# Row 0 of a fused attention and feed-forward kernel: two interleaved halves, masks added to the scores in PSUM, constants, casts and loads dealt out anew

## The chip, the cores and the metric

The kernel runs on one NeuronCore of a Trainium2 chip. The core has TensorE (PE, with its weight loads written PEld), VectorE (DVE), ScalarE (ACT), GpSimd (POOL) and SyncE (SP), and 16 DMA engines. Times are device microseconds (us) of one execution; lower is better. The number of a kernel is the median of its runs.

## The reference, cut to what matters

Eight batch rows of 576 tokens go through attention with 8 heads of width 64. Heads 0 to 3 see a plain window of 32 tokens back, heads 4 to 7 see every fourth token of the last 128. The result, 4608 tokens of width 512, goes through a feed-forward layer of width 2048 with a squared ReLU.

```python
scores = np.matmul(q, k.transpose(0, 1, 3, 2)) / np.sqrt(D)      # B, H, S, D = 8, 8, 576, 64
rel = pos[:, None] - pos[None, :]
mask_plain = (rel >= 0) & (rel < 32)                             # heads 0..3
mask_dil = (rel >= 0) & (rel < 128) & (rel % 4 == 0)             # heads 4..7
scores = np.where(masks[None], scores, -1e9)
attn = softmax(scores); x = np.matmul(attn, v)                   # -> 4608 tokens x 512
h = np.maximum(x @ w_in, 0.0)                                    # 512 -> 2048
out = (h * h) @ w_out                                            # 2048 -> 512, float32
```

All inputs and the output are float32 in DRAM; the kernel computes with float16 operands and accumulates in float32.

## The kernel before, in words

The feed-forward layer is done in nine chunks of 512 tokens. A chunk needs the transposed attention output `xT` of its tokens, so chunk c needs attention rows up to c. The order of all instructions is written out by hand: `pending` holds generators that emit feed-forward matmuls a few at a time, and `pump(n)` emits the next n pieces between two pieces of attention. Each engine then works through its own queue in that order.

Attention row 0 has no feed-forward work to go with it. Its q and k of the sliding heads are loaded as float32 into `sq` (q on SP's queue, k on ACT's, 1.5 KB runs), its q and k of the dilated heads through POOL's DMA queue, which casts to float16 on the way, straight into `nd_`, its v into `sv` and `sd`. The steps after that: casts (`cast_sliding_qk`), transposes on PE and copies out of PSUM (`t_sliding`, `t_dilated`), scores (`s_sliding`, `s_dilated`), exp on ACT and a multiplication with a 0/1 mask on DVE (`softmax`), the product with v and the normalization (`av_sliding`, `av_dilated`, `normalize`), and transposes into `xT` (`x_sliding`, `x_dilated`). `idle_matmuls` on a zero tile `zz` (14 wide ones at the start, then 5 narrow ones at each step) fill PE's time. Row 0 is laid out as whole tiles of 576 columns; its second half (`av_dilated(0, 1, a)`, `x_sliding(0, 1)`, `x_dilated(0, 1)`) is put between the first pieces of chunk 0.

Chunk 0 is done in two parts in its first layer (`mm1_part_gen`, tokens 0 to 287 at L302, then 288 to 511), and row by row in its second (`mm2_by_rows_gen`, L345). Attention row 1 runs inside chunk 0, with the same steps as row 0: its casts at L145 and L147, then transposes and scores, then `cast_v`, then `attn_values`. The chunks 1 to 8 are `moe_gen`: `mm1_gen` (L324) and a Strassen form of the second layer (`mm2_strassen_gen`, L374); the rows 2 to 7 run inside them, with q and k of those rows first copied to DRAM as float16 (`keep_qk`, L184) and then transposed by DMA on SP's queue (`transpose_by_dma`, L194 and L196) into `QKTx` and `QKTd`.

The loads of row 1 and of the weights are held back: `load_w_in` (two pieces of 1 MB, L128) after the third step of row 0, `load_sliding_qk(1)` and `load_dilated_qk(1)` after the last step that reads row 0's tiles, `load_w_out` (four pieces of 0.5 MB, L135) after the first part of chunk 0's first layer, `reload_v(1)` (L106, L113, L114) after that part, `keep_qk(2)` after row 1's scores. What holds them back is a memset of a part of the tile that is to be loaded, or of the scratch column `hold`, at the wanted place of an engine's queue. The pool `pa` has two PSUM tiles (scores and products with v take turns in them), the pool `pm` four.

The masks are built at L220 to L231, other constants at L232 to L246.

Of the kernel before, what the change touches and what calls it, by code (L numbers as in the profile page):

```python
# [17 lines left out]
def kernel(  # L18
# [58 lines left out]
    QKTp = const.tile([P, 2, 2, PADP + S], FP16, name="QKTp")  # L77
# [9 lines left out]
    early = tp.tile([QB, 2, 2, 12 * D * 2], FP16, name="early", tag="T")  # L87
    nq_ = early[:, 0].rearrange("p i (j h d) -> p i j h d", j=6, h=HH)
    nd_ = early[:, 1].rearrange("p i (g x) -> p i g x", g=2)
# [12 lines left out]
    def load_sliding_v(b):  # L102
        for m in range(NB):
            lo = QB * m - PADP
            p0 = PADP if m == 0 else 0
            nc.sync.dma_start(  # L106
                out=sv[p0:P, m, :, :],
                in_=v[b, 0:HH, lo + p0 : lo + P, :].transpose([1, 0, 2]),
            )

    def load_dilated_v(b, eng):
        vv = v[b, HH:H].rearrange("h (i c) d -> i h (c d)", c=DIL)
        eng.dma_start(out=sd[PADD:P, 0, :, :], in_=vv[0:QD])  # L113
        eng.dma_start(out=sd[:, 1, :, :], in_=vv[QD - PADD : CL])  # L114
# [11 lines left out]
    def load_w_in():  # L126
        for f0, f1 in ((0, 1024), (1024, 2048)):
# [5 lines left out]
    def load_w_out():  # L133
        for j in range(4):
# [23 lines left out]

    def cast_sliding_v(eng, step, m0=0, m1=NB):
        for m in range(m0, m1, step):  # L160
            copy(eng, vp[:, m : m + step, :, 0:D], sv[:, m : m + step, :, :])

    def cast_dilated_v(eng, step):
        for t in range(2):
# [37 lines left out]
    load_sliding_qk(0, (nc.sync, nc.scalar))  # L202
# [7 lines left out]
    nc.vector.memset(sd[0:64, 0, :, :], 0.0)  # L210
    nc.scalar.activation(warm, warm, ACTF.Exp)
    load_dilated_qk(0)
    make_identity(nc, ident)
    load_sliding_v(0)
    load_dilated_v(0, nc.scalar)
# [4 lines left out]
    for m, w, pad in ((maskp, QB, PADP), (maskd, QD, PADD)):  # L220
# [6 lines left out]
        nc.vector.tensor_mul(  # L227
            m.rearrange("p (n w) -> p n w", w=w),
            lo_[:, 0:w].unsqueeze(1).to_broadcast([P, UW // w, w]),
            hi_[:, 0:w].unsqueeze(1).to_broadcast([P, UW // w, w]),  # L230
        )  # L231
    nc.vector.memset(QKTp[:, 1, :, 0:PADP], 0.0)  # L232
    nc.vector.memset(QKTx[:, 1, 0:PADP], 0.0)
    nc.vector.memset(QKTd[:, 1, :, 0:KPAD], 0.0)
    nc.vector.memset(AT[:, :, UW:640], 0.0)

    nc.vector.memset(vp[:, :, :, D : D + 1], 1.0)
    nc.vector.memset(vp[0:PADP, 0, :, D : D + 1], 0.0)
    nc.vector.memset(vd[:, 1, :, :, D : D + 1], 1.0)
    nc.vector.tensor_scalar(  # L240
        out=vd[:, 0, :, :, D],
        in0=relf[:, 0:1].unsqueeze(2).to_broadcast([P, DIL, HH]),
        scalar1=-PADD + 0.5,
        scalar2=None,
        op0=ALU.is_lt,
    )  # L246
# [249 lines left out]
    def t_sliding(b, hp, i, wide=False):  # L496
        p_ = pt(f"pt{b}_{hp}_{i}", wide)
        for j in range(6):
# [7 lines left out]
            QKTp[:, i, hp, PADP:].rearrange("x (p j) -> x p j", j=6),  # L506
# [19 lines left out]

    def softmax(u, ps, mask):
# [3 lines left out]
    def s_sliding(b, hp):  # L531
        tiles = [pa(f"ps{b}_{hp}_{half}") for half in range(2)]
        for half, ps in enumerate(tiles):
            for m3 in range(3):
                m = 3 * half + m3
                for e in range(2):
# [3 lines left out]
                        QKTp[r, 1, hp, QB * m : QB * m + P],  # L540
                        QKTp[r, 0, hp, PADP + QB * m : PADP + QB * (m + 1)],
# [43 lines left out]
    def normalize(b, what, pav, w):  # L585
        x = xp.tile([QB, 2, HH, D], FP16, name=f"x{b}_{what}", tag="x")
        rcp = xp.tile([QB, 2, HH], FP32, name=f"rcp{b}_{what}", tag="rcp")
        pv = pav[0:w, :, 0 : HH * (D + 2)].rearrange("p i (h d) -> p i h d", d=D + 2)
        nc.vector.reciprocal(rcp[0:w], pv[:, :, :, D])
        nc.vector.tensor_tensor(  # L590
            out=x[0:w],
            in0=pv[:, :, :, 0:D],
            in1=rcp[0:w].unsqueeze(3).to_broadcast([w, 2, HH, D]),
            op=ALU.mult,
        )
        return x

    def av_sliding(b, mp):
        pav = pa(f"pav{b}_{mp}")
        for i in range(2):  # L600
            m = 2 * mp + i
# [12 lines left out]
        return normalize(b, f"p{mp}", pav, QB)  # L614

    def av_dilated(b, t, a):
        pav = pa(f"paw{b}_{t}_{a}")
        for e in range(2):
            for h in range(HH):
                off = e * 288 + a * 144 + t * QD  # L620
                nc.tensor.matmul(  # L621
                    pav[:, e, h * (D + 2) : h * (D + 2) + D + 1],
                    AT[:, 4 + h, off : off + P],
# [6 lines left out]
    def x_sliding(b, half, xs, wide):  # L630
        px = pt(f"px{b}_{half}", wide)
        for m3 in range(3):
            m = 3 * half + m3
            x = xs[m // 2][:, m % 2].rearrange("p h d -> p (h d)")
# [12 lines left out]
    def x_dilated(b, t, xs, wide):  # L647
        py = pt(f"py{b}_{t}", wide)
        for a in range(2):
            for e in range(2):  # L650
                x = xs[a][:, e].rearrange("p h d -> p (h d)")
# [30 lines left out]
    def attn_values(b, fill, wide=False):  # L682
        xs = []
        for mp in range(3):
            xs.append(av_sliding(b, mp))
# [3 lines left out]
        ys = [av_dilated(b, 0, 0)]  # L689
# [3 lines left out]
        ys.append(av_dilated(b, 0, 1))  # L693
        fill()
        zs = []
        for a in range(2):
            zs.append(av_dilated(b, 1, a))
# [7 lines left out]
    cast_sliding_qk(0, (nc.scalar, nc.scalar, nc.vector, nc.gpsimd))  # L705
    pj = pmool.tile([P, TOKC], FP32, name="pj", tag="pm")
    idle_matmuls(pj, 14, TOKC)

    def idle():
        idle_matmuls(pj, 5, P)  # L710

    def idle_and_load():
        idle()
        n_idle[0] += 1
        if n_idle[0] == 3:

            nc.vector.memset(hold, 0.0)
            nc.gpsimd.memset(hold, 0.0)
            load_w_in()
            cast_sliding_v(nc.gpsimd, 2)  # L720

    n_idle = [0]
    transposes_and_scores(0, idle_and_load)
    scores_dilated(0, idle)
    cast_dilated_v(nc.scalar, DIL)
    xs = [av_sliding(0, 0)]
    idle()
    xs.append(av_sliding(0, 1))

    nc.vector.memset(sq[:, :, :, 0:1], 0.0)  # L730
    nc.vector.memset(nd_[:, :, :, 0:1], 0.0)
    idle()
    ys = [av_dilated(0, 0, 0)]
    idle()
    x_sliding(0, 0, xs, False)
    idle()
    ys.append(av_dilated(0, 0, 1))
    idle()
# [124 lines left out]
```

The softmax here doesn't subtract the row's maximum and nothing guards it: scores larger than these inputs give would overflow.

## Time and profile before

| | us |
|---|---|
| median of 11 runs | 307.21 (306.31 to 308.09) |
| the profiled execution, its own time | 307.57 |
| its span, from the first to the last instruction | 305.8 |
| PE busy | 294.5 (96%) |
| DVE busy | 213.8 (70%) |
| ACT busy | 184.7 (60%) |
| POOL busy | 42.2 (14%) |
| first matmul of chunk 0's first layer (L302) starts at | 23.75 |
| first matmul of chunk 1's first layer (L324) starts at | 63.47 |

A profile line of the timeline gives the start, the busy time in us, the engine, the line of the kernel, the operation, its output and inputs with shapes, the count, and in brackets how long the engine was idle before it and on what. A line of a table by stage gives the length of the stage, then for each engine the busy time and the number of instructions, then the clock that PE was granted (1.00 is full speed), the share of DMA engine time and GB/s. A line of a DMA queue gives packets, MB written, and the time of the packets as a share of the 16 engines' time. DMA sizes are those of the destination; a load that casts float32 to float16 reads twice as much.

### The profile page before, as it was taken

To read this page: it belongs to the slowest core of one execution; us is meant where nothing else is said; L and a number is where in the kernel's file an instruction comes from. 1 tells how busy PE (TensorE), PEld (TensorE's weight loads), DVE (VectorE), ACT (ScalarE), POOL (GpSimd) and SP (SyncE) were. 2 spreads that over 40 slices of the span, in tenths; PEclk is the share of its full clock that TensorE was granted. 3 is DMA by queue.
4 is the path that set the end of the run, shared out by engine and by line. 5 is a ranking of instruction groups with operands and counts; after the bars stand their busy time and mean duration, and the time that the engine had idled before them with its cause. 6 is when DMAs were issued, how large, how long until landed. Compare 5 with 4: busy or idle time off the path is not lost.

```text
span 305.8 us, 7069 instructions
## 1 busy us (share of the span) xinstructions
PE 294.5 (96%) x2920; PEld 198.1 (65%) x2920; DVE 213.8 (70%) x428; ACT 184.7 (60%) x317; POOL 42.2 (14%) x86
## 2 busy tenths in 40 slices
PE   7789999999899999999999999999999999999995
PEld 2777774444696469646974597459745974684484
DVE  5496772579975797669776977697769775834744
ACT  2586983768924893489438943894389536405710
POOL 4422302006003200320032002300100010000000
PEclk9799999999999999999999999999999999999999
DMA  7999899799899989899859993988420012003004
GB/s 186 245 212 241 143 187 241 165 223 272 206 178 250 263 115 230 238 196 186 192 146 211 168 226 117 223 197 190 118 77 2 0 52 87 2 0 140 0 0 139
DMA packets 83313, 47.91 MB, mean 157 GB/s; under 512 B 67793, under 2 KB 79569, under 8 KB 82897
## 3 DMA queue, kind: packets, MB, share of 16 engines
q1 hardware_dynamic: 75060, 26.12, 40.8%
q0 software_dynamic: 6848, 19.80, 28.5%
q10 hardware_dynamic: 1372, 1.54, 1.8%
q8 instruction: 23, 0.38, 0.5%
q14 instruction: 10, 0.07, 0.1%
HBM read 39.85 MB, written 16.52 MB: 184 GB/s over the span
## 4 chain that ended last, share of the span: by engine, by line
PE 86%; DMA 6%; ACT 3%; SPq 2%; DVE 1%; issue 1%; DVEq 0%; ACTq 0%
PE ph L324 37%; PE pob L374 9%; PE poa L374 9%; PE poe L374 5%; PE poc L374 5%; PE pod L374 5%; DMA sv<-in_v_dram 3%; PE paw L621 3%; PE ph L302 3%; SPq L106 2%; DMA sq<-in_k_dram 2%; PE pav L607 2%; PE py L654 2%; PE pj L474 2%; PE pz L575 1%; PE px L636 1%
## 5 line engine op out<-in xcount | busy, mean ns | idle before, releaser
L324 PE MATMUL ph<-xT,wi 128*128 128x512 f16 x512 | 115.8, 379 | 0.0
L290 ACT ACTIVATE rt<-ph 128x512 f16<-128x512 f32 x128 | 75.4, 601 | 32.9 <-PE ph L324 32.6
L324 PEld LDWEIGHTS <-wi 128*128 128x128 f16 x512 | 48.2, 98 | 55.0
L294 DVE TENSOR_TENSOR g<-rt 128x1024 f16<-128x1024 f16 x56 | 38.7, 691 | 35.2 <-ACT rt L290 34.9
L374 PEld LDWEIGHTS <-sm 128*128 128x128 f16 x512 | 46.9, 98 | 4.9
L374 PEld LDWEIGHTS <-g 128*128 128x128 f16 x384 | 35.8, 98 | 6.5 <-DVE g L292 1.1
L374 PE MATMUL pob<-T,sm 128*128 128x256 f16 x256 | 32.5, 272 | 0.0
L374 PE MATMUL poa<-wo,g 128*128 128x256 f16 x256 | 32.1, 273 | 0.0
L660 ACT COPY xT<-py 128x576 f16<-128x576 f16 x16 | 10.2, 639 | 25.8 <-PE py L654 25.6
L394 POOL DMA_DIRECT2D out_dram<-otl x6 | 4.5, 753 | 152.3 <-DVE otl L429 152.3
L590 DVE TENSOR_TENSOR x_d<-paw,rcp_d 72x512 f16<-72x512 f32 x32 | 22.0, 687 | 1.1
L528 ACT ACTIVATE AT<-pz 128x576 f16<-128x576 f32 x32 | 19.1, 650 | 2.3 <-PE pz L575 1.8
L528 ACT ACTIVATE AT<-ps 128x576 f16<-128x576 f32 x32 | 19.2, 658 | 0.4
L642 ACT COPY xT<-px 128x576 f16<-128x576 f16 x16 | 10.3, 641 | 14.6 <-PE px L636 14.6
L529 DVE TENSOR_TENSOR AT<-AT,maskp 128x576 f16<-128x576 f16 x32 | 15.2, 480 | 3.4 <-ACT AT L528 2.4
L302 PE MATMUL ph<-xT,wi 128*128 128x288 f16 (+1 forms) x128 | 16.6, 272 | 0.9 <-ACT xT L660 0.5
L590 DVE TENSOR_TENSOR x_p<-pav,rcp_p 96x512 f16<-96x512 f32 x24 | 16.5, 686 | 0.8
L529 DVE TENSOR_TENSOR AT<-AT,maskd 128x576 f16<-128x576 f16 x32 | 14.1, 456 | 3.4 <-ACT AT L528 2.5
L374 PE MATMUL poc<-T,sm 128*128 128x256 f16 x128 | 16.2, 272 | 0.0
L374 PE MATMUL pod<-T,g 128*128 128x256 f16 x128 | 16.2, 272 | 0.0
L374 PE MATMUL poe<-wo,sm 128*128 128x256 f16 x128 | 16.1, 273 | 0.0
L345 PE MATMUL po<-wo,g 128*128 128x512 f16 x64 | 16.1, 379 | 0.0
(99 smaller groups left out, 368.4 us busy)
## 6 DMA issues: line engine op xcount, KB each, us to landing
sv<-in_v_dram SPq DMA_DIRECT2D x40, 128.0 KB, 4.2
sd<-in_v_dram SPq DMA_DIRECT2D x7, 512.0 KB, 5.8
dk<-in_k_dram POOLq DMA_DIRECT2D x12, 288.0 KB, 6.3
dk<-in_q_dram POOLq DMA_DIRECT2D x12, 288.0 KB, 7.6
out_dram<-otl POOLq DMA_DIRECT2D x6, 512.0 KB, 3.5
out_dram<-otu POOLq DMA_DIRECT2D x6, 512.0 KB, 3.7
wi<-in_moe_w_in_dram POOLq DMA_DIRECT2D x2, 1024.0 KB, 12.6
wo<-in_moe_w_out_dram POOLq DMA_DIRECT2D x4, 512.0 KB, 10.1
```

The lines of the kernel that those rows point to most:

```text
L290: nc.scalar.activation(rt[:, o, :], ph[:], ACTF.Relu)
L294: nc.vector.tensor_mul(g[:, ffc - 1 : ffc + 1, :], rt, rt)
L302: nc.tensor.matmul(ph[:, 0 : t1 - t0], wi[:, dmk, ffc * P : ffc * P + P], xs[:, dmk, :], start=(dmk == 0), stop=(dmk == NDM - 1),)
L324: nc.tensor.matmul(ph, wi[:, dmk, ffc * P : ffc * P + P], xs[:, dmk, :], start=(dmk == 0), stop=(dmk == NDM - 1),)
L345: nc.tensor.matmul(po, g[:, ffc, t * P : (t + 1) * P], wo[:, ffc, :], start=(ffc == 0), stop=(ffc == NFF - 1),)
L374: nc.tensor.matmul(acc, lhs[:, k, t * P : (t + 1) * P], rhs[:, k, :], start=(first and k == 0), stop=(k == NK - 1), skip_group_check=True,)
L528: nc.scalar.activation(AT[:, u, 0:UW], ps[:, :, 0 : UW // 2], ACTF.Exp, scale=scale)
L529: nc.vector.tensor_mul(AT[:, u, 0:UW], AT[:, u, 0:UW], mask)
L590: nc.vector.tensor_tensor(out=x[0:w], in0=pv[:, :, :, 0:D], in1=rcp[0:w].unsqueeze(3).to_broadcast([w, 2, HH, D]), op=ALU.mult,)
L621: nc.tensor.matmul(pav[:, e, h * (D + 2) : h * (D + 2) + D + 1], AT[:, 4 + h, off : off + P], vd[:, t, 2 * a + e, h, 0 : D + 1], start=Tru ...
L642: nc.scalar.copy(xT[:, 0:2, t0 : t0 + 288], px[:, 0:UW].rearrange("x (c t) -> x c t", c=2),)
L660: nc.scalar.copy(xT[:, 2:4, t0 : t0 + 288].rearrange("x c (i r) -> x c i r", r=DIL), py[:, 0:UW].rearrange("x (c r i) -> x c i r", c=2, r= ...
```

## The change

Row 0 is cut into two halves of 288 tokens (index f). Each half has its own loads, casts, transposes, scores and products, and the halves are interleaved by hand; all of row 0 now comes before chunk 0. Chunk 0's first layer is done with `mm1_gen`, 512 columns wide, instead of two parts.

The masks of row 0 are no longer multiplied in. For each score tile two matmuls of the identity with `biasp` or `biasd` (0 where the mask is 1, -30000 where it is 0) write PSUM first, the scores are accumulated on top, and ACT's exp gives zero. Rows 1 to 7 keep the multiplication.

Some constants (zeros of `sd` and `QKTd`) are written by ACT, others (`constants()`) come later on DVE; casts of v and one cast of q go to POOL. `w_in` is loaded in four pieces of 512 columns, two after POOL's cast of q and two after its casts of v. The loads of row 1, the rest of `w_out` and `keep_qk(2)` are held back by POOL alone: `landed(x)` is a POOL copy of one element of what a DMA wrote. Row 1's scores of the sliding heads and its dilated transposes move from the first into the second layer of chunk 0.

```diff
+    def load_sliding_qk_half(i, f, eng):
+        eng.dma_start(out=sq[:, i, :, 192 * f : 192 * (f + 1)], in_=...)   # runs of 768 B
+    def load_dilated_qk_half(f):
+        for i, src in ((1, k), (0, q)):
+            s4 = src[0, HH:H, 288 * f : 288 * (f + 1), :].rearrange("(g e) (p j) d -> e p g (j d)", e=2, j=8)
+            for e in range(2):
+                nc.gpsimd.dma_start(out=ndh[36 * e : 36 * (e + 1), f, i, :, :], in_=s4[e])
...
-    def load_w_in():
-        for f0, f1 in ((0, 1024), (1024, 2048)):
+    def load_w_in(j0, j1):
+        for f0, f1 in [(512 * j, 512 * (j + 1)) for j in range(j0, j1)]:
             nc.gpsimd.dma_start(out=wi[:, :, f0:f1], in_=moe_w_in[:, f0:f1]...)
...
-    load_sliding_qk(0, (nc.sync, nc.scalar))
+    load_sliding_qk_half(0, 0, nc.sync)
+    load_sliding_qk_half(1, 0, nc.scalar)
...
-    nc.vector.memset(sd[0:64, 0, :, :], 0.0)
     nc.scalar.activation(warm, warm, ACTF.Exp)
-    load_dilated_qk(0)
+    for hh in range(0, HH, 2):
+        nc.scalar.copy(sd[0:PADD, 0, hh : hh + 2, :], zz[0:PADD]...)
+    nc.scalar.copy(QKTd[:, 1, 0, :], zz[:, 0:1].to_broadcast([P, KPAD + S]))
+    nc.scalar.copy(QKTd[:, 1, 1, :], zz[:, 0:1].to_broadcast([P, KPAD + S]))
+    load_dilated_qk_half(0)
+    load_sliding_v(0, 0, 3)
+    load_dilated_v(0, nc.sync, (0,))
+    load_sliding_qk_half(1, 1, nc.sync)
+    load_sliding_qk_half(0, 1, nc.sync)
+    load_dilated_v(0, nc.sync, (1,))
+    load_sliding_v(0, 3, 6)
     make_identity(nc, ident)
-    load_sliding_v(0)
-    load_dilated_v(0, nc.scalar)
+    load_dilated_qk_half(1)
...
+        nc.vector.tensor_mul(m[:, 0:w], lo_[:, 0:w], hi_[:, 0:w])
+        nc.vector.tensor_scalar(out=bias..., in0=m..., scalar1=30000.0, scalar2=-30000.0, op0=ALU.mult, op1=ALU.add)
...
+    def biased(name, bias):
+        ps = pa(name)
+        for e in range(2):
+            nc.tensor.matmul(ps[:, e, 0 : UW // 2], ident, bias, start=True, stop=False, skip_group_check=True)
+        return ps
+    def exp_only(u, ps):
+        nc.scalar.activation(AT[:, u, 0:UW], ps[:, :, 0 : UW // 2], ACTF.Exp, scale=scale)
...
-    idle_matmuls(pj, 14, TOKC)
+    idle_matmuls(pj, 18, TOKC)
+    cast_sliding_qk_half(1, 0, nc.scalar)
+    cast_sliding_qk_half(0, 0, nc.vector)
+    t_sliding_half(0, 0, nc.scalar)
+    t_sliding_half(1, 0, nc.vector)
+    constants()
+    idle(8)
+    t_dilated_half(1, 0, nc.scalar)
+    s_sliding_half(0, 0)
+    s_sliding_half(1, 0)
+    idle(16)
+    t_dilated_half(0, 0, nc.vector)
+    idle(12)
+    s_dilated_half(0, 0)
+    s_dilated_half(0, 1)
+    t_dilated_half(1, 1, nc.scalar)
+    t_dilated_half(0, 1, nc.scalar)
+    cast_sliding_v(nc.gpsimd, 3, 0, 3)
+    cast_dilated_v(nc.gpsimd, DIL, (0,))
+    xs = av_sliding(0, 0, 2)
+    idle(8)
+    ys = av_dilated(0, 0, 0)
+    ys += av_dilated(0, 0, 1)
+    xs += av_sliding(0, 2, 3)
+    cast_sliding_qk_half(1, 1, nc.scalar)
+    cast_sliding_qk_half(0, 1, nc.gpsimd)
+    load_w_in(0, 2)
+    idle(8)
+    s_dilated_half(1, 0)
+    t_sliding_half(0, 1, nc.scalar)
+    t_sliding_half(1, 1, nc.vector)
+    s_dilated_half(1, 1)
+    idle(6)
     x_sliding(0, 0, xs, False)
     x_dilated(0, 0, ys, False)
+    s_sliding_half(0, 1)
+    s_sliding_half(1, 1)
+    cast_dilated_v(nc.gpsimd, DIL, (1,))
+    cast_sliding_v(nc.gpsimd, 3, 3, 6)
+    load_w_in(2, 4)
+    idle(8)
+    zs = av_dilated(0, 1, 0)
+    zs += av_dilated(0, 1, 1)
+    xs += av_sliding(0, 3, 5)
+    xs += av_sliding(0, 5, 6)
+    idle(12)
+    x_dilated(0, 1, zs, False)
+    idle(16)
+    x_sliding(0, 1, xs, False)
+    idle(12)
+    load_w_out(0, 1)
+    landed(wi[:, NDM - 1, 1023:1024])
+    nc.gpsimd.memset(sq[:, :, :, 0:1], 0.0)
     load_sliding_qk(1)
     load_dilated_qk(1)
+    load_w_out(1, 4)
+    landed(wo[:, 3, DM - 1 :])
+    nc.gpsimd.memset(sv[:, :, :, 0:1], 0.0)
+    nc.gpsimd.memset(sd[:, :, :, 0:1], 0.0)
+    load_v(1)
+    landed(wo[:, NFF - 1, DM - 1 :])
+    landed(sd[:, 1, HH - 1, DIL * D - 1 :])
+    dk = keep_qk(2)
     g0 = hidden(0)
-    pending.append(mm1_part_gen(0, g0, 0, 288))
...
+    pending.append(mm1_gen(0, g0))
+    pump(22)
+    cast_sliding_qk(1, (nc.scalar, nc.vector, nc.scalar, nc.vector))
     pump(2)
+    for hp in range(2):
+        for i in (1, 0):
+            t_sliding(1, hp, i)
+            pump(1)
     pump(1000)
+    pending.append(mm2_by_rows_gen(0, g0))
+    for g in range(2):
+        s_sliding(1, g)
+        pump(3)
+    pump(3)
+    for g in range(2):
+        for i in (1, 0):
+            t_dilated(1, g, i, True)
+            pump(1)
+    scores_dilated(1, lambda: pump(3))
+    cast_v(nc.scalar)
+    pump(2)
...
             for _ in weight_sums():                       # inside the loop over rows, b == 2
                 pump(2)
+            pump(2)
```

## The prediction

> **What bounds the kernel now.** I read the chain that ended last, then the timeline of the first 90 us, then the DMA queues in short windows.
>
> ```profile
> PE 86%; DMA 6%; ACT 3%; SPq 2%; DVE 1%; issue 1%; DVEq 0%; ACTq 0%
> ```
>
> From 63.47 us on the chain is PE without gaps (one wait of 0.9 us at 82, then the tail), and the change leaves that work as it is. So it is decided before: when does chunk 1 start?
>
> ```profile
> 0.74 7.47 DMA sq<-in_k_dram
> ...
> 23.75 0.41 PE L302 MATMUL ph<-xT,wi 128*128 128x288 f16 x2
> ...
> 22.28 0.43 SPq L97 DMA_DIRECT2D sq<-in_k_dram  x1
> ...
> 34.87 1.55 ACT L145 CAST early<-sq 96x768 f16<-96x768 f32 x2
> ...
> 53.26 1.47 ACT L145 CAST vp<-sv 128x1536 f16<-128x1536 f32 x1 [4.21 <-DMA sv<-in_v_dram]
> ...
> 63.47 7.52 PE L324 MATMUL ph<-xT,wi 128*128 128x512 f16 x34
> ```
>
> Row 0's k lands at 8.2, chunk 0 starts at 23.75, row 1's sq (asked for at 22.3, landed 34.4) is cast at 34.87, row 1's v at 53.26, chunk 1 starts at 63.47. Chunk 0 and row 1 are 35.7 us of pure PE work in these 39.7 (below); loads and hand-overs take the rest. The queues show the price of a packet:
>
> ```profile
> q0 software_dynamic: 208, 0.42, 112.0%
> ...
> q0 software_dynamic: 321, 0.31, 107.1%
> ...
> q0 software_dynamic: 309, 0.32, 92.7%
> q1 hardware_dynamic: 310, 0.08, 29.6%
> ```
>
> Each row is a 2 us window. At 22 to 24 us w_in is alone, 4 KB read per packet: 104 packets/us, 0.21 MB/us. At 36 to 38 w_out is alone, 2 KB read per packet: 160 packets/us, but only 0.155 MB/us. At 42 to 44 two queues run together: equal numbers of packets, whatever their size.
>
> **Part by part.**
>
> *Row 0's start.* q and k of half 0 are 0.58 MB instead of 1.15. Before, 0.49 MB had moved by 4.0 us and 0.27 MB/us after; q's last packet went at about 5.7 and it landed at 7.44. So half 0's last packet goes at about 4.6 and it lands near 6.1, two us sooner. ACT gets new work ahead of its cast: two copies of 512 (0.6 each) and two of 640 (0.7), from 2.7 to 5.3; hidden, as 6.1 is later. DVE loses a memset of 0.91 and keeps the masks: hidden too. But PE has 18 wide idle matmuls in its queue: 0.427 each until about 5.9, then 0.216, from 1.23 to 7.4. Transposes start at 7.4 instead of 9.24, and at full speed: before, the clock was at half from 9.3 to 12.7.
>
> *Row 0's middle.* POOL's casting loads sent their first packet only at 6 us, and with sv's packets gone by then they share with sd and then with the second q and k. At about 100 packets/us each, the 144 packets of dilated k land at 9.2, q at 10.6, the second half at 12.0 and 13.4 (1.5 us from last packet to landing). PE waits from 8.4 to 9.2 for the first. Then: dilated k 0.3, two biased sliding scores 0.95 to 10.45, 16 idle 0.9, dilated q 0.3, DVE copies 0.45+0.81 to 12.6, first dilated exp on ACT 13.1. The chain is then ACT's queue: 8 exp and copies of about 0.61 to 0.70 (4.95), 4 half copies at 0.35 (1.4), the cast 0.83, small waits 0.9: 21.2. Then DVE's four normalizations, 3x0.89+0.65, to 24.6; transposes 0.45, ACT's copy 0.64, so chunk 0 starts at **25.8** (24.0 to 27.0).
>
> *The masks.* Removed: 8 multiplications on DVE, 4.4 us busy, which each stood between exp and the product with v. Added: 16 matmuls of 288 columns, 0.12 each (64 of them took 7.8 us in chunk 0), 1.9 us of PE, of which the chain above holds 0.25 per tile. Idle matmuls pay for the rest; without that cover 1.9 is the price. An exp over biased scores is taken as 0.61, as L528; PSUM start and accumulate may add nothing or 0.1 per tile. DVE's 288-wide bias ops: 0.2 (lo_) to 0.5 (maskp), hidden under the load.
>
> *POOL.* Casts of 768 and 1024 columns: from the cast 96x768 (0.82) and vp's 128x512 (0.61 to 0.80) I take 0.9 and 1.3, bounds 0.8 to 1.6; waits for v end before. Its cast of the second q waits for that load: SP's queue has 384+1408+288+384+384 packets up to it, last one at 13.3, landed 14.6. Only then, at 15.5, come the first two w_in issues (0.77 each). Before they went at 12.77.
>
> *w_in in four pieces.* 512 columns are packets of 2 KB read, as w_out's. The Trainium skill, "DMA: Bandwidth & Descriptors", Specifications, puts full rate at 512 B and more, by which cutting runs from 4 to 2 KB is free: 1 MB in 4.9 us at w_in's present rate. The trace says 0.155 instead of 0.21 MB/us: 6.6 us. By the page row 1's loads start 1.7 us earlier. I take the trace. First packet 2.3 us after issue (as before: 12.8 to 15.1), so 17.8 to 24.4, landed 25.8.
>
> *Row 1's q and k.* `landed(wi)` keeps POOL, and with it SP's loads into sq, until then; behind it in POOL's queue stand the dilated loads, three of w_out, and v. A POOL copy (0.3 to 0.7, as L803) and a memset: issue at 26.6 instead of 21.85. 768 packets beside w_in and w_out at 85 to 90 packets/us (before: 183 packets/us for both queues) take 8.8, after about 1.8 of start: last packet 37.0, landed **38.2**. The casts stand behind the 11th block of mm1, 25.8+11x0.863+0.7 = 36.0. So ACT and DVE wait 2.2, with the relu of the next block queued behind ACT's cast, and PE, whose four PSUM tiles fill, with them.
>
> *From the cast to chunk 1.* Before: 34.87 to 63.47, 28.6, with v late at 53.26. After: PE still has 16 matmuls of mm1 (3.45), 4 transposes at 0.26, 64 of the second layer at 0.216 (13.8), 4 score tiles at 0.47, 4 dilated transposes, 7 products and 4 output transposes at 0.26: 24.1. On top: ACT must do two casts, five relu and two copies (5.9) for it, 1.6 PE can't hide; waits for the two pa tiles 1.0; cast_v after the last exp, now 5 pumps behind the scores instead of 15: 0.8. Sum 27.5: chunk 1 at **65.7**. v's loads start when w_out's first piece has landed (about 39.6) and share packet by packet with the rest: sv 53.5, sd 56.7, wanted at 55.5 and 57.0, so no more than 0.3. keep_qk(2) waits for that, 57.3 instead of 49.9; before, QKTx was there 16.2 us after (66.06); after, at 73.5, wanted at 65.7+8.2 = 73.9. No stall, with 0.4 to spare; the two extra pumps buy it.
>
> *Chunk 0's first layer.* 64 matmuls of 512 at 0.216 are 13.8; the two parts were 7.8+6.3. Gain 0.3, contained above. PE's pure work of before: 14.1 + 13.8 + row 1 6.8 + the rest of row 0 1.0 = 35.7.
>
> Sum: 65.7 - 63.25 (its first weight load) = +2.4; the span 305.8 becomes 308.2, the profiled time 307.57 becomes 310.0. That execution lies 0.36 above the median, so against the median: 307.2 + 2.4 = **309.6**. About 0.2% (0.6 us) is what a measurement of this kernel can tell from no change.
>
> **The rivals.**
>
> *A, faster.* Row 0 is ready at 24.0 and sq lands before 34.5, so nothing waits: chunk 1 is at 24.0 + 10.2 (to the casts) + 27.5 = 61.7. That is -1.5, 305.7. For it: POOL's loads may start sooner than at 6 us, and w_in may run at its old rate and be asked for at 14. Against: three rows above. It decides if sq lands before 35.7.
>
> *B, no load late, row 0 as forecast.* 25.8 + 10.2 + 27.5 = 63.5: +0.3, 307.5, which is no change.
>
> *C, much slower: PE goes cold while it waits for sq.*
>
> ```profile
> 7.00:8.00 1.00, 0.00 (x0) 1.00 1.19 220
> 8.00:9.00 1.00, 0.00 (x0) 1.00 1.19 233
> 9.00:10.00 1.00, 0.76 (x10) 0.68 1.14 232
> 10.00:11.00 1.00, 1.00 (x14) 0.50 1.18 228
> 11.00:12.00 1.00, 1.00 (x14) 0.50 1.13 247
> 12.00:13.00 1.00, 1.00 (x15) 0.62 1.15 254
> ```
>
> Fifth column: the granted clock. A gap of 2.5 us (6.74 to 9.24) was enough for 3.4 us at half speed. The skill's "TensorE: Matmul & The Clock Gate", Why this matters for your kernels, wants gaps over 3 us for that; by it the 2.2 of my sum cost nothing, by this row up to 1.7. I leave it out of the sum and keep it in the range: +4.1, and with v or QKTx 1 us late +5, 312.
>
> *D, no effect of the bias.* If DVE's masks were hidden anyway, row 0 gains nothing from it; the forecast gives it no gain of its own, since ACT's queue sets row 0.
>
> **How the numbers follow.** Forecast (sq late by 1 to 3.5) 0.55, own range 308.4 to 311.0; A 0.21; B 0.14, two thirds of it within 0.2% and the rest slower; C 0.10. Faster 0.21; same 0.09; slower 0.55+0.05+0.10 = 0.70. The range 305.9 to 311.8 leaves out the lower third of A and the upper part of C, under 2 in 10.
>
> **What would show it.** First matmul of L378 near 25.8; w_in's queue at about 155 packets/us; sq issued near 26.6, its cast on ACT waiting on DMA sq for about 2 us; chunk 1 near 65.7; from there the same span. It is wrong if that cast waits for nothing, or if chunk 1 starts before 63.

## The result, and the profile after

The changed kernel takes 309.42 us (median of 12 executions, 308.44 to 311.54) against 307.26 for the kernel before on the same chip (47 executions): the ratio is 1.0076, with a 95% interval of 1.0059 to 1.0093. It is slower by about 2.2 us. The two profiled executions differ by less: 309.3 against 307.57, and 307.5 against 305.8 from the first to the last instruction. The profile before lies 0.3 above the median of its kernel, the profile after 0.1 below.

First, the stages of the two kernels: to the first matmul of chunk 0, to the casts of row 1, to the first weight load of chunk 1, to the end. Columns: the stretch and its length, then busy time and instructions of PE, PEld, DVE, ACT and POOL, the granted clock, the DMA share and GB/s. Before:

```profile
0.00:23.75 23.75, 19.00 (x262) 13.86 (x263) 15.78 (x47) 12.73 (x21) 9.26 (x21) 0.93 1.04 214
23.75:34.87 11.12, 10.64 (x115) 8.88 (x114) 6.26 (x15) 8.99 (x22) 3.21 (x7) 1.00 0.93 200
34.87:63.25 28.38, 27.00 (x300) 16.07 (x299) 17.23 (x45) 18.75 (x40) 2.77 (x6) 1.00 1.08 197
63.25:305.80 242.55, 237.88 (x2250) 159.31 (x2248) 174.54 (x325) 144.23 (x236) 26.98 (x54) 1.00 0.63 144
```

After:

```profile
0.00:26.44 26.44, 22.69 (x336) 15.70 (x337) 12.75 (x43) 15.60 (x28) 16.56 (x31) 1.00 1.08 195
26.44:37.68 11.24, 10.52 (x48) 4.60 (x47) 3.46 (x6) 6.57 (x11) 2.93 (x7) 1.00 1.16 244
37.68:64.64 26.96, 25.32 (x267) 12.99 (x268) 17.16 (x38) 18.31 (x31) 2.37 (x6) 1.00 0.90 171
64.64:307.50 242.86, 237.88 (x2250) 159.34 (x2248) 174.93 (x325) 144.27 (x236) 26.68 (x54) 1.00 0.64 146
```

Chunk 0 starts 2.69 later, the next stage is 0.12 longer and the third 1.42 shorter, so chunk 1 starts 1.39 later. Between chunk 0 and chunk 1 PE is busy for 35.84 instead of 37.64 and idle for 2.36 instead of 1.86. So 1.80 of PE's work is no longer there (row 0's second half now comes ahead of chunk 0, and the first layer is done in one part), half a us of waiting was added, and chunk 0's start went back by more than was gained. From chunk 1 on PE's work is the same (237.88 in both) but takes 0.31 longer. Most of that is one longer wait of PE, for ACT's cast of row 2's v, here before and after:

```profile
82.01 0.41 PE L607 MATMUL pav<-vp,AT 128*128 128x65 f16 x8 [0.91 <-ACT vp L145]
...
84.65 0.42 PE L745 MATMUL pav<-vp,AT 128*128 128x65 f16 x8 [1.17 <-ACT vp L166]
```

The chain that ended last has less PE and more DMA:

```profile
PE 84%; DMA 9%; ACT 2%; SPq 1%; issue 1%; POOL 1%; DVE 0%; ACTq 0%; POOLq 0%
...
0.74 4.80 DMA sq<-in_k_dram
...
24.24 13.41 DMA sq<-in_k_dram
```

Columns are start and length. Its largest new piece is the last line: row 1's k, asked for at 24.24, takes 13.41 us to land. The timeline shows what stands on both sides of it:

```profile
7.26 0.68 PE L585 MATMUL ph<-ident,early 96*128 96x96 f16 x12
...
14.74 0.42 PE L603 MATMUL pg<-ident,early 72*128 72x72 f16 x8 [1.15 <-DMA early<-in_q_dram]
...
15.20 0.70 ACT L166 COPY QKTd<-pg 128x288 f16<-128x288 f16 x2 [0.69 <-PE pg L603]
...
17.97 0.65 ACT L685 ACTIVATE AT<-pz 128x576 f16<-128x576 f32 x1 [1.35 <-PE pz L711]
...
23.55 0.19 POOL L854 CAST hold<-wi 128x1 f32<-128x1 f16 x1 [1.95 <-DMA wi<-in_moe_w_in_dram]
...
23.80 0.33 SPq L100 DMA_DIRECT2D sq<-in_q_dram  x1
...
26.44 10.52 PE L378 MATMUL ph<-xT,wi 128*128 128x512 f16 x48
...
37.73 1.56 ACT L166 CAST early<-sq 96x768 f16<-96x768 f32 x2 [1.00 <-DMA sq<-in_k_dram]
38.62 0.43 PE L553 MATMUL pt<-ident,early 96*128 96x96 f16 x6 [1.66 <-ACT early L166]
...
54.65 1.47 ACT L166 CAST vp<-sv 128x1536 f16<-128x1536 f32 x1
...
64.86 1.48 PE L378 MATMUL ph<-xT,wi 128*128 128x512 f16 x6
```

Row 0's transposes start two us sooner than before (7.26 against 9.24), but everything gained is gone by 26.44. `landed(wi)`, POOL's wait for the first half of w_in, ends at 23.55, and row 1's q is asked for at 23.80. Row 1's casts on ACT wait 1.00 for the DMA, and PE 1.66 for the cast. Row 1's v is cast at 54.65 without a wait, where it waited 4.21 before. The queues, in 2 us from 18, from 28 and from 38 us:

```profile
q0 software_dynamic: 410, 0.42, 125.6%
...
q0 software_dynamic: 203, 0.19, 62.2%
q1 hardware_dynamic: 198, 0.30, 49.2%
...
q0 software_dynamic: 414, 0.41, 124.2%
```

At 18 w_in is alone, now with packets that read 2 KB: 205 packets/us, 0.21 MB/us, the same bytes as before with packets twice the size. At 28 w_in and sq run with equal numbers of packets, 100/us each. At 38 w_out is alone and also moves 0.21 MB/us.

### The profile page after: what moved, and what is told of

Its sections match the earlier page's. It is cut to its first block, busy times and chain, and to the rows that moved or that the text cites. A ratio compares the mean times of both kernels' runs of the same rounds, so it can differ in the third digit from the quotient of the medians.

```text
span 307.5 us, 7006 instructions
## 1 busy us (share of the span) xinstructions
PE 296.4 (96%) x2900; PEld 192.6 (63%) x2900; DVE 208.3 (68%) x409; ACT 184.7 (60%) x305; POOL 48.5 (16%) x97
## 4 chain that ended last, share of the span: by engine, by line
PE 84%; DMA 9%; ACT 2%; SPq 1%; issue 1%; POOL 1%; DVE 0%; ACTq 0%; POOLq 0%
PE ph L378 38%; PE pob L428 9%; PE poa L428 9%; DMA sq<-in_k_dram 6%; PE poe L428 5%; PE poc L428 5%; PE pod L428 4%; PE po L399 4%; DMA sv<-in_v_dram 3%; PE paw L762 2%; PE pav L745 2%; PE pz L665 2%; PE ps L646 1%; PE py L795 1%; PE px L777 1%; SPq L125 1%
## 5 line engine op out<-in xcount | busy, mean ns | idle before, releaser
L378 PE MATMUL ph<-xT,wi 128*128 128x512 f16 x576 | 130.5, 379 | 0.1
L344 ACT ACTIVATE rt<-ph 128x512 f16<-128x512 f32 x144 | 85.0, 601 | 36.2 <-PE ph L378 35.9
L378 PEld LDWEIGHTS <-wi 128*128 128x128 f16 x576 | 54.3, 98 | 61.8 <-issue 0.2
L348 DVE TENSOR_TENSOR g<-rt 128x1024 f16<-128x1024 f16 x63 | 43.6, 692 | 44.3 <-ACT rt L344 44.1
L801 ACT COPY xT<-py 128x576 f16<-128x576 f16 x16 | 10.2, 640 | 27.6 <-PE py L795 27.5
L783 ACT COPY xT<-px 128x576 f16<-128x576 f16 x16 | 10.3, 641 | 13.4 <-PE px L777 13.4
L618 ACT ACTIVATE AT<-pz 128x576 f16<-128x576 f32 x28 | 16.7, 649 | 1.9 <-PE pz L665 1.5
L726 DVE TENSOR_TENSOR x_p<-pav,rcp_p 96x512 f16<-96x512 f32 (+1 forms) x25 | 16.6, 665 | 0.9
L618 ACT ACTIVATE AT<-ps 128x576 f16<-128x576 f32 x28 | 16.7, 649 | 0.8 <-PE ps L628 0.3
L725 DVE RECIPROCAL rcp_d<-paw 72x8 f32<-72x8 f32 x32 | 6.3, 198 | 15.7 <-PE paw L762 15.7
L468 ACT COPY otu<-poa 128x512 f32<-128x512 f32 x8 | 4.7, 586 | 17.5 <-PE poa L428 17.5
L528 PE MATMUL pj<-zz 128*128 128x128 f16 (+1 forms) x124 | 13.8, 263 | 1.2 <-DVE zz L237 1.2
```

Of the source, the lines that this page charges most:

```text
L344: nc.scalar.activation(rt[:, o, :], ph[:], ACTF.Relu)
L348: nc.vector.tensor_mul(g[:, ffc - 1 : ffc + 1, :], rt, rt)
L378: nc.tensor.matmul(ph, wi[:, dmk, ffc * P : ffc * P + P], xs[:, dmk, :], start=(dmk == 0), stop=(dmk == NDM - 1),)
L528: nc.tensor.matmul(pj[:, 0:cols], zz[:, 0:P], zz[:, 0:cols], start=True, stop=True)
L618: nc.scalar.activation(AT[:, u, 0:UW], ps[:, :, 0 : UW // 2], ACTF.Exp, scale=scale)
L725: nc.vector.reciprocal(rcp[0:w, 0:n], pv[:, :, :, D])
```

## The experiments

The theory: chunk 1 comes a fixed time after row 1's casts, and these start at the later of two moments, sq's landing, and chunk 0's start plus 10.2. After the change both are late: sq because `landed(wi)` holds it, chunk 0 because of row 0. The rivals: the clock that falls in a wait, the masks, and a bound further on that makes an earlier start worthless. Each kernel in the table is the changed one with the edit named. The first four columns come from one profiled execution each, the last from all executions of the kernel.

ACT casts two of row 1's four pieces, k's and then q's. They run back to back, the second 0.7 later, except in the rows with a star: there k is loaded first, and the start and the wait given are those of the second cast. The fourth column counts from the second cast in every row.

| kernel | chunk 0 | row 1's casts start on ACT (waited for sq) | chunk 1 | from ACT's second cast to chunk 1 | ratio to before, interval |
|---|---|---|---|---|---|
| after | 26.44 | 37.73 (1.0) | 64.86 | 26.4 | 1.0076, 1.0059 to 1.0093 |
| sq freed from w_in | 27.55 | 37.73 (0) | 64.78 | 26.3 | 1.0052, 1.0036 to 1.0067 |
| k first | 27.72 | 37.90 (0) | 64.96 | 26.3 | 1.0050, 1.0028 to 1.0072 |
| sq freed, PE kept busy in row 0 | 26.55 | 36.74 (0) | 63.79 | 26.3 | 1.0029, 1.0014 to 1.0044 |
| k first, PE kept busy in row 0 | 26.86 | 39.29* (1.4) | 67.03 | 27.7 | 1.0080, 1.0055 to 1.0105 |
| first products ahead of late transposes | 26.33 | 38.52 (1.9) | 67.03 | 27.8 | 1.0131, 1.0094 to 1.0167 |
| masks multiplied in | 28.04 | 38.23 (0) | 65.28 | 26.3 | 1.0064, 1.0040 to 1.0088 |
| w_in in two pieces | 26.51 | 39.84 (3.0) | 68.35 | 27.8 | 1.0101, 1.0068 to 1.0135 |
| w_in in two pieces, PE kept busy | 26.48 | 38.93 (2.2) | 66.65 | 27.0 | 1.0119, 1.0093 to 1.0146 |
| chunk 0 in two parts, k first | 21.37 | 39.22* (3.1) | 67.76 | 28.5 | 1.0081, 1.0043 to 1.0120 |
| chunk 0 in two parts, k first, sq freed | 21.07 | 37.37 (0) | 64.63 | 26.5 | 1.0092, 1.0065 to 1.0118 |
| w_in asked for early | 35.89 | 46.08 (0) | 73.13 | 26.3 | 1.0308, 1.0280 to 1.0337 |
| w_in early, two parts, k first | 20.96 | 45.25* (0.9) | 71.47 | 26.2 | 1.0237, 1.0208 to 1.0267 |

Three profiled executions are not typical of their kernels: that of "sq freed, PE kept busy in row 0" has a span of 310.1 where the median is 306.5, that of "k first, PE kept busy in row 0" 309.6 where it is 308.0, and that of "w_in in two pieces" 310.9 where it is 308.8. In the expectations, e1_k_first is the kernel with k first, e2_sq_free that with sq freed and e6_wi_1024 that with w_in in two pieces.

**sq freed from w_in.** POOL's wait ahead of row 1's loads is left out:

```diff
     load_w_out(0, 1)
-    landed(wi[:, NDM - 1, 1023:1024])
     nc.gpsimd.memset(sq[:, :, :, 0:1], 0.0)
```

> Row 1's loads into sq are no longer held until half of w_in has landed; POOL goes on after its last issue of w_in and w_out. Theory 1: sq is asked for at about 21.8 instead of 23.8, lands near 35.5, before the casts want it (36.6), so they wait for nothing: chunk 1 1.0 sooner, span 306.5. Rival (packets are shared one by one, so an earlier start only slows w_in): w_in's later pieces arrive after PE wants them (30 and 33.4), PE waits in the first layer instead, and chunk 1 stays within 0.3 of 65.0.

sq is asked for at 21.91, its last packets go before 35.0, and no cast waits for it. But chunk 0 starts at 27.55 in this execution, so the casts start where they did. The clock shows why (PE alone, one us from 13 to 20: length, busy time and count, granted clock, DMA share, GB/s):

```profile
13.00:14.00 1.00, 0.56 (x16) 1.00 1.11 201
14.00:15.00 1.00, 0.19 (x6) 1.00 1.14 275
15.00:16.00 1.00, 1.00 (x25) 0.76 1.36 262
16.00:17.00 1.00, 1.00 (x20) 0.50 0.46 80
...
19.00:20.00 1.00, 1.00 (x24) 1.00 1.21 203
```

PE waits 1.2 us for the second dilated q, and then gets half the clock for 3.4 us. The 19 executions of this kernel fall into two groups: 12 with a mean clock of 0.991 to 0.994 and spans of 307.3 to 308.2, 7 with 0.998 to 1.000 and spans of 306.3 to 306.7. Of the changed kernel, six executions have 0.998 to 1.000, and their spans are 306.7 to 308.0, median 307.45 against 306.4. So where the clock does not fall, freeing sq is worth about 1.0 us, as theory 1 had it (306.5). The kernels with idle matmuls, below, test whether the clock takes it back in the other group.

**Row 1's k first.** In row 1's load of sq, k goes ahead of q; `landed(wi)` stays.

```diff
-    load_sliding_qk(1)
+    for i in (1, 0):
+        nc.sync.dma_start(out=sq[:, i, :, :], in_=(q, k)[i][1, 0:HH].rearrange("h (p j) d -> p h (j d)", j=6))
```

> Row 1's k is loaded ahead of its q, all else as in the changed kernel. Theory 1 (the casts of row 1 wait 1.0 us for the k that is loaded second, and PE with them): k lands about 4 us sooner, near 33.5, the casts of k start at 36.6 instead of 37.7, those of q follow with at most 0.2 of wait; chunk 1 starts 0.8 to 1.0 sooner than 64.98, span 306.6, ratio to the kernel before 1.0045 instead of 1.0076. Rival (the wait is covered elsewhere, by v or by ACT's queue): chunk 1 stays at 65.0, span 307.5.

The casts wait for nothing, but again after a row 0 with a wait of 1.6 us and half the clock (chunk 0 at 27.72). The ratio is nearly that of the kernel with sq freed.

**sq freed, and PE kept busy in row 0.** With `landed(wi)` left out as above:

```diff
     t_dilated_half(1, 1, nc.scalar)
+    idle(20)
     t_dilated_half(0, 1, nc.scalar)
```

> As the run that freed sq from w_in (sq issued 21.9, landed 33.8), with 20 more idle matmuls between the two dilated transposes of row 0, so that PE's clock doesn't fall there. Theory (chunk 1 comes 27.3 us after the later of sq's landing and chunk 0's start + 10.2): chunk 0 at 26.5 to 26.9, casts at about 36.8 and waiting for nothing, chunk 1 at 64.0 to 64.2, span 306.6, ratio 1.003. If chunk 0's start doesn't set it (rival: PE's work between chunk 0 and chunk 1 and the share of the DMA engines give the same end whatever starts early), chunk 1 stays at 64.8 and the ratio at 1.005.

What the theory expected came, chunk 1 a little sooner than 64.0:

```profile
26.55 10.52 PE L378 MATMUL ph<-xT,wi 128*128 128x512 f16 x48
...
36.74 1.55 ACT L166 CAST early<-sq 96x768 f16<-96x768 f32 x2
...
63.79 8.38 PE L378 MATMUL ph<-xT,wi 128*128 128x512 f16 x38
```

Of 22 executions 21 have a mean clock of 0.997 or more, and 19 of them spans of 306.2 to 307.1. (The profiled one is the other, at 312.0: in it a piece of row 2's v took 14.2 us to land, at 75.5, after all that the table shows. The ratio rests on the 22.) This interval and that of the changed kernel do not touch: sq's lateness and the clock in row 0 together are worth 0.47%, 1.4 us of the 2.3 that the ratio of the changed kernel makes. What is left, 0.29%, is 0.9 us. In the profiles chunk 1 is 0.32 late (63.79 against 63.47), which is row 0's later end less the PE work taken out of chunk 0. The rest comes after chunk 1 or is chance between executions, and no run places it; the longer wait for row 2's v (0.3 in the changed kernel) is a part at most.

**k first, and PE kept busy.** The same idle matmuls with k first and `landed(wi)` in place:

```diff
     t_dilated_half(1, 1, nc.scalar)
+    idle(20)
...
-    load_sliding_qk(1)
+    for i in (1, 0):
+        nc.sync.dma_start(out=sq[:, i, :, :], in_=(q, k)[i][1, 0:HH]...)
```

> e1_k_first with 20 narrow idle matmuls (1.1 us) in the wait for the dilated q of the second half, where the clock fell to half in e1_k_first and e2_sq_free (15 to 20 us, chunk 0 1.2 later). Theory 1 and 2 together: the clock stays at 1.00, chunk 0 starts near 26.5, the casts of k do not wait for the load and start at 36.6, chunk 1 near 64.0, span 306.5, ratio 1.003 to 1.005. Rival (the load still binds): casts at 37.7 with a wait for DMA, span 307.5.

Row 0 is as forecast, with the clock at 1.00, but w_in lands a us later in this execution, at 24.70, so sq's q lands only at 39.2. The casts of k start at 36.93 and wait for nothing; those of q wait 1.4, and PE behind them 1.9, after which its clock is at 0.50 from 42 to 44. The five executions that were not profiled have a mean clock of 0.999 or 1.000 and spans of 307.3 to 308.3, as the changed kernel has. So keeping row 0's clock up gained nothing here; that the load decides is seen in the one profile and is likely, not shown, for the others.

**The first products ahead of the late transposes.** ACT's copies of the second dilated half are put behind the first products with v.

```diff
-    t_dilated_half(1, 1, nc.scalar)
-    t_dilated_half(0, 1, nc.scalar)
...
     xs += av_sliding(0, 2, 3)
+    t_dilated_half(1, 1, nc.scalar)
+    t_dilated_half(0, 1, nc.scalar)
     cast_sliding_qk_half(1, 1, nc.scalar)
```

> The transposes of the dilated second half (which waited 1.2 us for their load, at 14.7) are put behind the first half's products with v. Theory 1 (two limits in a row: row 0 and then sq's landing at 37.65): chunk 0 starts about 1.0 sooner, at 25.4, but the casts still start at 37.7 and wait 2.0 instead of 1.0, so chunk 1 stays at 65.0 and the span at 307.5 (plus or minus 0.3). Rival (row 0's length alone makes the change slower): the gain of 1.0 is kept, span 306.5.

A miss for row 0: chunk 0 starts at 26.33, not a us earlier, because ACT's cast of the second k moves back to 16.85 and PE waits 0.4 for it. w_in's first half lands at 24.41, sq is asked for 0.86 later than in the changed kernel, and the casts wait 1.9 to 2.0. PE then waits 2.55, and now the clock does fall; the 2 us from 38 and those from 42:

```profile
38.00:40.00 2.00, 0.59 (x8) 1.00 1.23 206
...
42.00:44.00 2.00, 2.00 (x11) 0.50 1.22 197
```

In the changed kernel, with a wait of 1.66 there, it does not:

```profile
38.00:40.00 2.00, 1.38 (x16) 1.00 1.24 207
...
42.00:44.00 2.00, 2.00 (x21) 1.00 1.22 196
```

From the second cast to chunk 1 it takes 27.8 instead of 26.4. So the wait costs itself and 1.4 more.

**w_in in two pieces, without and with idle matmuls.** First the pieces of before, of 1024 columns:

```diff
-        for f0, f1 in [(512 * j, 512 * (j + 1)) for j in range(j0, j1)]:
+        for f0, f1 in [(512 * j0, 512 * j1)]:
```

> w_in in two pieces of 1024 columns (4 KB read per packet) in place of four of 512 (2 KB). My forecast had 0.155 MB/us for 2 KB packets; the trace of the changed kernel shows about 206 packets/us, 0.205 MB/us. If packet size does not matter from 2 KB up: w_in's first MB lands within 0.5 of 23.5, and while sq shares with it packet by packet, 4 KB packets slow sq: it lands later, near 39 instead of 37.65, chunk 1 up to 1 later. If 4 KB packets were cheaper per byte: the first MB lands 1 us sooner, sq at 36.5, chunk 1 sooner by 1.

Then the same, with 12 wide idle matmuls ahead of row 1's transposes, where PE would wait for sq:

```diff
     cast_sliding_qk(1, (nc.scalar, nc.vector, nc.scalar, nc.vector))
-    pump(2)
+    pump(1)
+    pw = pmool.tile([P, TOKC], FP32, name="pw", tag="pm")
+    pump(1)
+    idle_matmuls(pw, 12, TOKC)
```

> w_in in two pieces as in e6_wi_1024 (there PE waited 3.7 us for row 1's cast, then worked at half the clock until about 44.5), with 12 wide idle matmuls (2.6 us) in that wait. Theory 2 (the wait costs a second time because the clock drops after it): the granted clock stays at 1.00 in 40 to 45, the casts start at 39.8 as before, and chunk 1 starts 1.0 to 1.7 sooner than 68.35. Rival (the half clock is hidden by ACT, which has casts, relu and copies to do): chunk 1 stays within 0.3 of 68.35.

Pieces of 1024 columns are no faster: the first MB lands at 24.28, against 23.55 for two pieces of 512.

```profile
24.28 0.19 POOL L854 CAST hold<-wi 128x1 f32<-128x1 f16 x1 [3.72 <-DMA wi<-in_moe_w_in_dram]
```

That settles the packet size: 2 KB per packet costs w_in nothing. Here sq landed latest of the kernels whose row 0 and w_in keep their places, the casts waited 3.0 and PE 3.7, and the clock fell (0.50 from 42 to 44). With the idle matmuls the clock stays at 1.00 from 36 to 46, and from the second cast to chunk 1 it takes 27.0 instead of 27.8. The timed ratios of the two don't differ within their intervals; their own waits for sq differ by 0.8 in the profiles, so this pair sizes the fall of the clock only roughly.

**Masks multiplied in.** Row 0's two identity matmuls per tile are taken out and DVE's multiplication is put back, all else stays.

```diff
     def biased(name, bias):
-        ps = pa(name)
...
+        return pa(name)
     def exp_only(u, ps):
-        nc.scalar.activation(AT[:, u, 0:UW], ps[:, :, 0 : UW // 2], ACTF.Exp, scale=scale)
+        softmax(u, ps, maskp if u < 4 else maskd)
...
-                    start=False,
+                    start=True,
```

> The changed kernel with row 0's masks multiplied in on DVE again (8 multiplications of 576 columns, 0.46 to 0.48 each) and the 16 bias matmuls taken out. Theory (ACT's queue, loads and PSUM turns set row 0, the masks were hidden): chunk 0 starts within 0.5 of 26.44, the casts of row 1 still start when k has landed (37.65), span 307.2 to 307.8, ratio within 0.002 of the changed kernel's 1.0076. Rival (the mask sits between exp and the product with v, so taking it out shortens row 0): chunk 0 starts 1 to 2 later and the ratio rises to 1.010 or more.

DVE has the masks again (groups of L619), and PE's waits name it and the exp in front of it (engine, tile and line, what it waited for, then us in total, times, longest):

```profile
L619 DVE TENSOR_TENSOR AT<-AT,maskp 128x576 f16<-128x576 f16 x4 | 2.4, 616 | 1.5 <-ACT AT L618 1.3
L619 DVE TENSOR_TENSOR AT<-AT,maskd 128x576 f16<-128x576 f16 x4 | 1.8, 459 | 1.9 <-ACT AT L618 1.7
...
PE pav L738 <- DVE x_d L719: 0.9, 1, 0.9
PE paw L755 <- ACT AT L618: 0.7, 1, 0.7
```

4.2 us of DVE are back, and the ratio is 1.0064 against 1.0076, intervals overlapping: no difference that was measured. Chunk 0 starts at 28.04, later than the theory allowed and within what the rival named, but the half clock between 16 and 20 is in it; against the two kernels above with the same (27.55 and 27.72) it is 0.3 to 0.5 late. The mask in PSUM may be worth that much in row 0, and nothing of it shows in the ratio.

**Chunk 0 in two parts, its first part inside row 0.** As in the kernel before; with k first:

```diff
     load_w_in(2, 4)
-    idle(8)
+    g0 = hidden(0)
+    pending.append(mm1_part_gen(0, g0, 0, 288))
+    pump(1)
     zs = av_dilated(0, 1, 0)
...
-    pending.append(mm1_gen(0, g0))
-    pump(22)
+    pending.append(mm1_part_gen(0, g0, 288, TOKC))
+    pump(6)
```

> The changed kernel with k of row 1 loaded before q, and chunk 0's first layer in two parts again, its first part (288 tokens) started between the products of row 0's second half where idle matmuls stood. Theory 1 (all of row 0 ahead of chunk 0 leaves PE without useful work for 2.7 us of idle matmuls plus waits): the first matmul of chunk 0 is at about 22, the casts of row 1 start at 33.5 to 34.5 instead of 37.7, chunk 1 at 61.5 to 62.7, span 304 to 305.3, ratio 0.991 to 0.998: faster than both. Rival (row 0's halves and w_in's landing set the pace, not the place of chunk 0): w_in's first or third piece is late for the earlier start, PE waits for it, and the ratio stays at 1.003 or more.

Chunk 0 starts at 21.37, 2.4 earlier than before the change, and in the profiled execution it is worth nothing:

```profile
25.64 0.41 SPq L914 DMA_DIRECT2D sq<-in_q_dram  x1
...
35.26 0.82 ACT L166 CAST early<-sq 96x768 f16<-96x768 f32 x1
...
39.22 0.83 ACT L166 CAST early<-sq 96x768 f16<-96x768 f32 x1 [3.13 <-DMA sq<-in_q_dram]
```

k is cast at 35.26, the q behind it only at 39.22, and PE's clock is at 0.50 from 40 to 44. Row 1's q sets the time here, not row 0. This is one of two groups: five of the nine executions have spans of 308.9 to 310.4, the profiled one 310.2, and four have 306.2 to 306.5, better than any of the changed kernel (306.7 to 309.7) and as good as the best kernel of the table. None of the four was profiled, so whether q lands sooner in them, or the clock keeps up, is open.

**The same, with sq freed.**

```diff
-    landed(wi[:, NDM - 1, 1023:1024])
```

> Chunk 0's first layer in two parts (the first inside row 0's tail), row 1's k loaded ahead of its q, and sq freed from w_in (asked for at 22 instead of 25). Theory: sq's packets and those of w_in's second half now run at about equal numbers from 24 on, so sq's q lands at 34 to 35, but w_in's fourth piece lands near 33 instead of 30.5, and PE waits 2 to 3 us for it inside chunk 0's first part. Chunk 0's first matmul at 21.4, casts of row 1 at 34.5 to 35.5 without a wait, chunk 1 at 62.5 to 64, ratio 0.998 to 1.003: the loads of row 1 and of w_in can't both be early, and what one gains the other gives back. Rival: w_in isn't disturbed (last piece by 31) and chunk 1 comes at 61.5 to 62.5, ratio 0.994 to 0.997, faster than both kernels.

The loads trade places as expected: the casts wait for nothing, and PE waits inside chunk 0's first part instead.

```profile
PE ph L356 <- DMA wi<-in_moe_w_in_dram: 2.7, 1, 2.7
```

Chunk 1 is at 64.63, later than the forecast 62.5 to 64, and the ratio of 1.0092 misses it by more: the six executions have spans of 307.1 to 309.2, those with the lowest mean clock (0.989) 308.8. In the profiled one (307.1) the wait for w_in did not bring the clock down (PE alone):

```profile
31.00:33.00 2.00, 0.35 (x3) 1.00 1.16 265
33.00:35.00 2.00, 2.00 (x19) 1.00 1.21 211
```

The others were not profiled. This kernel beats neither the changed one nor the one before.

**w_in asked for early.** Its first two pieces go ahead of POOL's casts of row 0's v (issued at 7.22 instead of 15.45), the other two to where the first were.

```diff
     t_dilated_half(0, 1, nc.scalar)
+    load_w_in(0, 2)
     cast_sliding_v(nc.gpsimd, 3, 0, 3)
...
-    load_w_in(0, 2)
+    load_w_in(2, 4)
     idle(8)
```

> Only w_in's loads move: its first half goes ahead of POOL's casts of row 0's v (about 11 us instead of 15.5), its second half to where the first was. Theory: the first half lands by 20 instead of 23.6, sq is issued as soon as POOL is free, near 22, and lands by 34.5; the price is that row 0's second dilated q and the sliding halves share the DMA engines with w_in and land 0.5 to 1.5 us later, so chunk 0 starts at 26.5 to 28. Casts without a wait, chunk 1 27.3 us after them: 64.0 to 65.5, ratio 1.002 to 1.007. If row 0's loads are not disturbed, the lower end; if w_in's packets displace them packet for packet, the upper.

And this with chunk 0 in two parts and k first, as above (`mm1_part_gen` inside row 0's tail, the loop over `(1, 0)` in place of `load_sliding_qk(1)`).

> The early w_in of the run before, chunk 0's first layer in two parts as in the kernel before the change (its first part, of 288 tokens, runs inside the tail of row 0), and row 1's k loaded ahead of its q. Theory: chunk 0's first matmul at 21.4 to 22.5, no wait for w_in at 30, sq's q landed at about 35, casts there, PE's work of row 0's tail (1.0) hidden beside it: chunk 1 at 62.0 to 63.0, span 304.8 to 305.5, ratio 0.996 to 1.000. If the loads are what bounds (rival: sq's q still lands after 37, because w_in's second half, sq and w_out share the engines), chunk 1 is 27.3 to 28.5 after that, 64.5 or later, and the ratio 1.004 or more.

Both are far slower than expected, and for one reason. The second sliding half of v (packets of 256 B) goes out beside w_in. These are lines of the first of the two: of the waits, the timeline, and the queues from 20 to 22 us:

```profile
PE pav L745 <- POOL vp L168: 7.9, 1, 7.9
...
29.25 0.83 POOL L168 CAST vp<-sv 128x768 f16<-128x768 f32 x1 [8.75 <-DMA sv<-in_v_dram]
...
q0 software_dynamic: 320, 0.31, 91.7%
q1 hardware_dynamic: 325, 0.08, 30.4%
```

v moves 0.04 MB/us, one packet for each of w_in's, and lands at 29 instead of 18.5. In the changed kernel this queue runs alone at that stage: 1356 packets in the 2 us from 14. PE stands for 7.9 us and then works at half the clock nearly until chunk 0 starts (0.50 from 26 to 34), POOL and with it row 1's loads are late (sq asked for at 31.0), and chunk 0 starts at 35.89. In the second kernel PE stands for 7.5 us at the same place. So asking for w_in only at 15.5 keeps it out of row 0's v; a moment between 7.2 and 15.5 was not tried.

## Why the prediction was right, and where its steps were off

The forecast was 309.6 and +2.4; 309.42 was measured, +2.2 in the medians and +1.7 in the profiled spans. Its mechanism held: chunk 0 later, row 1's loads held until w_in lands, casts that wait for sq, little changed from chunk 1 on. That the final number is so close is in part luck. In the profiles chunk 1 came at 64.86 where 65.7 was forecast, two errors in the sum nearly cancel (below), and the medians differ by 0.4 more than the profiles. The sum also takes 65.7 for chunk 1's first matmul and subtracts 63.25, its first weight load before; with 63.47, the first matmul, it is +2.2 and 309.4. Its terms, one by one:

- Row 0's end: 25.8 forecast, 26.44 measured. The transposes start at 7.26 (forecast 7.4). The second dilated q landed at 14.7, not 13.4, and PE waits 1.15 for it. ACT, whose queue was to set row 0 with 0.9 of small waits, then waits 0.69 and 1.35 for PE's matmuls behind that q: this is the step that was too short. POOL's cast of q at 14.68 (forecast 14.6) and w_in's issue at 15.45 (15.5) came as forecast.
- w_in's packets: this term was mis-sized. The prediction took 0.155 MB/us for packets that read 2 KB, from w_out's row, over the Trainium skill ("DMA: Bandwidth & Descriptors", Specifications), by which runs of 2 KB have full rate. The changed kernel moved 0.205 MB/us, and the two-piece kernel was no faster. The page was right for w_in; the row of w_out was that of another transfer, and the same w_out moves 0.205 in the trace after. So the first half landed at 23.55, not 25.8, and sq was asked for at 23.80, not 26.6.
- sq's load: mis-sized the other way. From the first issue to the landing it took 13.85 us (13.41 from k's own issue), 11.6 were forecast. Its first packets went about 27.3, 3.5 us after the first issue instead of 1.8, and it landed 2 to 2.5 us after the last of its bulk instead of 1.2; in between it was faster, 100 packets/us instead of 85 to 90. (Two slips in that term are small: its own numbers put the last packet at 37.2, not 37.0, and before, both queues moved 163 packets/us from 24 to 32 us, not 183.) Two errors of 2.8 and 2.25 nearly cancel: sq landed at 37.65, forecast 38.2.
- The wait at the casts: 1.0 instead of 2.2, by 0.65 from chunk 0's later start and 0.55 from sq.
- From the first cast to chunk 1: 27.1, forecast 27.5. Counted from ACT's second cast, eight of the nine kernels of the table without a fall of the clock there have 26.2 to 26.5, the ninth, with 12 idle matmuls in that stretch, 27.0, and the four with a fall 27.7 to 28.5. v and `keep_qk(2)` caused no wait, as forecast; v's last landed at 53.9 (forecast 56.7). That PE would wait 0.26 longer for row 2's v, after chunk 1, was not in the sum.
- No gain from the masks of its own (rival D): so it was, within the interval.
- Rival C, a cold PE: not in the changed kernel's profile at this place, where a wait of 1.66 did not bring it. Waits of 1.9 (two together), 2.55, 3.0 and 3.7 us in four other kernels brought half speed, and with it 1.3 to 2.1 us more from the second cast to chunk 1. A wait of 2.75 in a fifth, with chunk 0 in two parts and sq freed, did not. So the page's 3 us is no safe limit, as the row of before (2.5 us) had said, but no length of the wait separates the two cases. What the prediction did not foresee is the same fall in row 0, at 15 us, after waits of 1.2 to 1.6.
- Rival A, faster: its condition "sq before 35.7" was made true by freeing sq. It wasn't enough, since chunk 0 stayed at 26.5 where A needed 24.0. With no load late chunk 1 is at 63.79, close to rival B's 63.5.

What halving row 0 could gain, then, went in two places. Row 0 really begins 2 us sooner, but its second dilated q lands only at 14.7, asked for behind the loads of the first half and v, and its second half, which before stood between matmuls of chunk 0, now stands ahead of them. And the wait on w_in pushes row 1's loads back by 1.96 (k asked for at 24.24 instead of 22.28). The second is shown by freeing sq. The first is read from the timeline: two kernels that put chunk 0's first part back into row 0 started chunk 0 at 21, but in their profiles lost the time again to waits for row 1's q or for w_in.

## What to carry to other kernels

Cutting the first row in halves moved its start, not its end, because the second half's loads came behind the first's: compute the landing of the last load before the gain of the first. An earlier start of a stage is worth something only if every load that it needs can be early too; freeing sq made w_in late where chunk 0 was early, and w_in asked for early made v late. Here two transfers of unequal packets shared the DMA engines packet by packet, so it paid to let the small packets through before a long load of large ones was started, as this kernel does with w_in and v. And a wait of PE can cost more than its length, 1.3 to 2.1 us more in four kernels here.

## What the runs showed of the hardware

- The share is by packets, not bytes: 320 and 325 packets in 2 us, 0.31 and 0.08 MB. The Trainium skill says so ("DMA: Bandwidth & Descriptors", Queues, rings and completion order: each engine takes turns between its queues packet by packet), and these rows agree, as far as the packets that the profile counts are the page's. Unexpected was the size: a piece of v, of 128 KB at most, took up to 19.2 us to land, where the median piece takes 3.2.
- PE's clock fell to half for about 3.4 us after a wait as short as 1.2 us (0.75 us busy in the 2 us from 13, sq freed). It did not after 1.66 us at 38 us in the changed kernel, after 1.3 us with only 0.68 us busy in the 2 us from 13 (w_in in two pieces, PE kept busy), or after 2.75 us at 30 us. With sq freed the mean clock is low in 12 of 19 executions, though only the profiled one shows where it fell. The skill's free-running window ("TensorE: Matmul & The Clock Gate", What's actually happening) fits a fall that depends on when the wait comes; its whole idle window of 3.4 us does not fit, since before these short falls no such window was idle.
- Why w_out, alone, moved 0.155 MB/us at 36 to 38 us in the kernel before, and 0.205 in the kernel after, is open.
